# Scores of two batches from float32r parts, and smaller work for the engines beside TensorE

## The chip, the cores and the metric

The kernel runs on one core of one Trainium2 chip. The metric is the device time of one execution in microseconds (us). A core has TensorE (PE in the profile; PEld is its weight load), VectorE (DVE), ScalarE (ACT), GpSimd (POOL) and the queue that issues transfers (SP). Each engine takes its own instructions strictly in the order in which the program lists them.

## The reference

```
scores = 0.125 * q @ k.T            # 4 batches x 8 heads, 576 x 576, head size 64, float32
thresh = max(scores) - tau          # by row
attn   = exp(where(scores >= thresh, scores, -1e9) - max)
attn   = attn / (sum(attn) + 1e-9)
x      = attn @ v                   # then 2304 tokens of 512
x      = moe(x, rms_norm)           # silu(xn @ w_gate) * (xn @ w_val) @ w_out, 512 -> 1536 -> 512
out    = moe2(x)                    # the same without the norm
```

The weights of the two feed-forward layers arrive as 64-bit floats.

## The kernel before, in words

The work of a batch is 36 score tiles (4 pairs of heads, 9 tiles of 128 query rows a pair; the fifth tile of a pair is made of two halves of 64 rows, one from each head) and then 36 units of feed-forward work of 48 matmuls each. A dense matmul is `128x128` weights against 288 columns, and float32 accuracy comes from three products of float32r parts (`dense`, L614): each operand is held as a rounded part and a remainder.

The program is not written in the order in which it runs. `op(...)` records each step with an engine, a planner's cost, what it reads and writes, and a priority; `Program.order` lists the steps by a simulation of its own, and the instructions are then issued in that list's order. The tables at the top (`NORM_E`, `V_E`, `OFF` and so on) choose which engine takes a step and how early it stands. The result is this: the 36 tiles of batch 0 run first, alone (the front, to about 110 us); then the dense units of batch b run with the tiles of batch b+1 between them; the units of the last batch run alone. Between batches stands the RMS norm: sums (L495), a short chain on DVE (`tok`, L500 to L510) and a spreading product (L518), which starts at 138.6 us for batch 0 and at 1009.9 us for batch 3.

One score tile goes through these lines: L388 `QK` (PE, float32 operands straight from `raw`, the transposed q and k, stored twice: partitions 0 to 63 and again 64 to 127; each half of the 576 columns uses one of the copies), L411 row maximum (DVE), L412 thresholds and bias from `K2`, which holds tau (DVE), L413 exponential (ACT), L414 mask and row sum (DVE), L420 and L421 two small steps on the sums (DVE), L426 reciprocal (DVE), L331/333/335 normalise (POOL, DVE or ACT by `NORM_E`), L346/348/350 the float16 part (by `HI_E`), L354/355 the remainder (by `LO_E`), L360 a transposing transfer, L447/450 the product with v. In the front the scores rotate over three PSUM tiles (`ps`), later they have one.

A weight unit (`weights`) is converted once, from 64 bits to 32, for each of 36 units in the front and under batch 0: three ACT steps (L581, L582, L583) and one DVE step (L584). Then L586 (ACT) and L588 (DVE or POOL) make the two parts. `q` and `qu` in L576 are every second 16-bit word of a scratch tile `t`.

## Time and profile before

| what | value |
|---|---|
| time, median of 3 runs | 1258.54 us (1257.33 to 1258.66) |
| the profiled execution | 1255.49 us |
| its span, first to last instruction | 1253.7 us |
| granted TensorE clock, mean | 0.98 |
| PE busy | 1186.2 us, 95% |
| DVE, ACT, POOL busy | 739.3, 625.2 and 393.0 us |

The profiled execution lasted 1.8 us more than its span. "Busy" of PE is the time in which a matmul was in flight; since matmuls are pipelined, the durations of single ones overlap, and the distance from start to start tells more.

### The profile page before, as it was taken

What the parts mean: (1) busy time and instruction counts of PE and PEld (TensorE: products, weight loads), DVE (VectorE), ACT (ScalarE), POOL (GpSimd) and SP (SyncE); (2) the same over time, 40 slices, a digit from 0 to 9 for tenths busy, and PEclk for the clock granted to TensorE, in tenths of its full rate; (3) what the DMA queues carried; (4) which work ended last, traced back from release to release, by engine and by line L of the source; (5) the groups of instructions that cost most, each with busy time, mean ns of one, the idle gap of its engine ahead of it and who ended that gap; (6) DMA issues with size and microseconds to landing.
All of it is one profiled execution on the core that took longest, in us unless ns stands there. A gap on an engine that the chain in (4) does not pass through costs nothing.

```text
span 1253.7 us, 21723 instructions
## 1 busy us (share of the span) xinstructions
PE 1186.2 (95%) x8528; PEld 1052.7 (84%) x8528; DVE 739.3 (59%) x1643; ACT 625.2 (50%) x875; POOL 393.0 (31%) x399
## 2 busy tenths in 40 slices
PE   4766799899999999999999999999999999999998
PEld 2334688788888988988889988889888999999998
DVE  7796787767778876566646566456545341233122
ACT  4789879999999644324333234333334212112211
POOL 3676434538443413222131243214232110001010
PEclk9787799999999999999999999999999999999999
DMA  8789679999999998768866677677656554444442
GB/s 236 165 180 218 229 235 276 287 292 293 306 293 282 300 291 189 197 188 197 197 197 188 177 207 188 195 196 178 174 168 175 161 175 167 167 168 168 168 168 106
DMA packets 225656, 261.48 MB, mean 209 GB/s; under 512 B 195985, under 2 KB 196497, under 8 KB 202513
## 3 DMA queue, kind: packets, MB, share of 16 engines
q1 hardware_dynamic: 225552, 260.09, 73.6%
q8 instruction: 67, 1.10, 0.3%
q14 instruction: 37, 0.29, 0.1%
HBM read 175.11 MB, written 42.47 MB: 174 GB/s over the span
## 4 chain that ended last, share of the span: by engine, by line
PE 83%; ACT 5%; DVE 3%; issue 1%; DMA 1%; POOL 0%; ACTq 0%; DVEq 0%; POOLq 0%
PE ps L614 71%; PE ps L388 5%; PE pt L447 4%; PE pt L450 2%; ACT t L581 1%; ACT t L583 1%; ACT t L582 1%; DVE w L584 1%; DMA ag<-e 1%; ACT w L586 0%; PE ps L518 0%; ACT e L346 0%; ACT e L413 0%; DVE e L414 0%; ACT e L335 0%
## 5 line engine op out<-in xcount | busy, mean ns | idle before, releaser
L614 PEld LDWEIGHTS ps<-XS,w 128*128 128x128 f32 x4608 | 619.9, 189 | 44.3 <-issue 30.8
L614 PE MATMUL ps<-XS,w 128*128 128x288 f32 x4608 | 648.5, 299 | 7.6 <-ACT XS L542 2.3
L614 PE MATMUL ps<-h,w 128*128 128x288 f32 x2304 | 322.6, 296 | 2.8 <-DVE Y L700 1.8
L614 PEld LDWEIGHTS ps<-h,w 128*128 128x128 f32 x2304 | 307.6, 188 | 19.9 <-issue 15.6
L411 DVE TENSOR_REDUCE col<-ps 128x1 f32<-128x576 f32 x144 | 107.9, 753 | 100.8 <-PE ps L388 100.3
L668 ACT CAST h<-th 128x576 fp32r<-128x576 f32 x96 | 64.5, 672 | 201.7 <-DVE th L664 201.6
L671 POOL TENSOR_TENSOR h<-th,h 128x576 fp32r<-128x576 f32 x45 | 65.7, 1459 | 298.4 <-ACT h L668 298.4
L653 DVE SCALAR_TENSOR_TENSOR th<-th,ps 128x576 f32<-128x576 f32 x94 | 70.7, 752 | 136.2 <-ACT th L652 136.1
L388 PE MATMUL ps<-raw 64*128 64x288 f32 (+1 forms) x640 | 115.1, 480 | 34.8 <-DVE Y L414 16.4
L414 DVE SCALAR_TENSOR_TENSOR e<-ps,col,e 128x576 f32<-128x576 f32 x126 | 102.5, 814 | 63.5 <-ACT e L413 63.1
L652 ACT ACTIVATE th<-ps 128x576 f32<-128x576 f32 x94 | 61.2, 651 | 134.0 <-PE ps L614 133.3
L413 ACT ACTIVATE e<-ps,col 128x576 f32<-128x576 f32 x126 | 92.9, 737 | 61.6 <-DVE col L412 60.6
L664 DVE SCALAR_TENSOR_TENSOR th<-th,ps 128x576 f32<-128x576 f32 x94 | 70.6, 751 | 58.7 <-PE ps L614 58.3
L447 PE MATMUL pt<-ag,v 128*128 128x256 f16 (+1 forms) x576 | 89.7, 306 | 15.9 <-DMA ag<-e 9.6
L388 PEld LDWEIGHTS ps<-raw 64*128 64x128 f32 (+1 forms) x640 | 45.8, 187 | 69.0 <-DVE Y L414 23.2
L447 PEld LDWEIGHTS <-v 128*128 128x128 bf16 x576 | 54.4, 103 | 43.0 <-issue 18.6
L354 POOL TENSOR_TENSOR e<-e,e 128x512 f16<-128x512 f32 x68 | 80.8, 1188 | 0.0
L355 POOL TENSOR_TENSOR e<-e,e 128x64 f16<-128x64 f32 x68 | 27.0, 397 | 160.1 <-ACT e L346 111.5
L700 DVE SCALAR_TENSOR_TENSOR Y<-ps,Y 128x576 f32<-128x576 f32 x64 | 48.2, 755 | 46.5 <-PE ps L614 45.6
L346 ACT CAST e<-e 128x576 f16<-128x576 f32 x88 | 58.6, 666 | 27.1 <-POOL e L331 15.1
L335 ACT ACTIVATE e<-e,col 128x576 f32<-128x576 f32 x72 | 61.8, 858 | 13.4 <-DVE col L426 13.2
L588 POOL TENSOR_TENSOR w<-w,w 128x1024 fp32r<-128x1024 f32 x20 | 48.3, 2415 | 55.7 <-ACT w L586 45.1
(87 smaller groups left out, 999.7 us busy)
## 6 DMA issues: line engine op xcount, KB each, us to landing
w<-kept SPq DMA_DIRECT2D x108, 1024.0 KB, 5.3
w<-in_w SPq DMA_DIRECT2D x36, 1024.0 KB, 6.9
kept<-w SPq DMA_DIRECT2D x36, 1024.0 KB, 7.1
raw<-in_qkv SPq DMA_DIRECT2D x31, 576.0 KB, 6.0
v<-in_qkv SPq DMA_DIRECT2D x32, 160.0 KB, 4.8
...
```

The source lines that it names most:

```text
L335: op("ACT", 865, lambda: nc.scalar.activation(e, e, AF.Identity, bias=c[:, 4:5], scale=c[:, 3:4]), **k)
L354: op(en, 670 if eng == 2 else 1170, lambda: n1.tensor_tensor(h[:, 640:], e[:, :512], h[:, :512], ALU.subtract), lock=True, w=[("lo", n)], ...
L388: nc.tensor.matmul(s[m:m + w, j, :HS], x[k, c0:c0 + w], x[k, S + j * HS:S + (j + 1) * HS], start=True, stop=True)
L411: op("DVE", 745, lambda: nc.vector.tensor_reduce(c[:, 0:1], s2, AX.XY, ALU.max, negate=True), w=[sk, ("mx", n)], bufs=[cb], p=T + F['MAX'] ...
L413: op("ACT", 738, lambda: nc.scalar.activation(e2, s2, AF.Exp, bias=c[:, 2:3], scale=SCALE), r=[("thr", n)], w=[sk, ("e", n)] + ek, bufs=[c ...
L414: op("DVE", 890, lambda: nc.vector.scalar_tensor_tensor(e2, s2, c[:, 1:2], e2, ALU.is_ge, ALU.mult, accum_out=c[:, 6:7]), r=[("thr", n)], ...
L447: nc.tensor.matmul(pv_[:, :w], v12[:, i if i < 5 else i - 5], o[:, i, :w], start=(i == 0), stop=False)
L614: nc.tensor.matmul(pt[:, j, :HS], w(i, a), x(i, b_)[:, j * HS:(j + 1) * HS], start=(i == 0 and a == 0 and b_ == 0), stop=(i == n - 1 and a ...
L653: op("DVE", 745, lambda: nc.vector.scalar_tensor_tensor(t2, t2, 1.0, g2, ALU.add, ALU.mult), lock=raw, w=gk + [("th", n)], bufs=[tb], p=T ...
L664: op("DVE", 745, lambda: nc.vector.scalar_tensor_tensor(t2, t2, 0.5, v2, ALU.mult, ALU.mult), lock=raw, w=vk + [("th", n)], bufs=[tb], p=T ...
L668: op("ACT", 672, lambda: nc.scalar.copy(h[:, 0], tb.t), r=[("th", n)], w=[("h0", n)], bufs=[tb, hb], p=T + 2 * U + DRAIN + OFF['HH'], name ...
L671: op(eng, 720 if eng == "DVE" else 1430, lambda: n1.tensor_tensor(h[:, 1], tb.t, f32(h[:, 0]), ALU.subtract), lock=True, r=[("th", n), ("h ...
```

## The change

For heads 16 to 31 (batches 2 and 3) q and k are split into float32r parts ahead of their tiles, as the dense operands are. A new tile `sp` holds the rounded q (both copies), the remainder of q, and for k the rounded part above the remainder. Three copies (L334 on ACT, L332 on POOL) and two subtractions (L338 and L339) make it, for each head. A full tile of scores is then four matmuls: two of all 128 rows (rounded q against rounded k and its remainder at once) and two of 64 rows (remainder of q against rounded k), in place of two float32 matmuls of 64 rows. The half tiles stay as they were.

Which engine subtracts is told by the variable `n1`, which the same function sets again for the split of v before the recorded step is issued; so the table `V_E` decides it, and in the order of instructions 8 heads have both subtractions on VectorE and 8 on GpSimd, where the planner's own table (`Q_E`) has 5 and 11. The copies stand where they were planned, 41 on ScalarE and 7 on GpSimd.

Further: tau's transfer and its constant stand first; the two small steps on the sums move from DVE to POOL for batches 0 and 1 (`S_E`); the first two conversion steps work on packed 16-bit words, in the low half of the unit's 32-bit tile `w32`, and only the third writes every second word of `t`, of which there is one instead of two; small tiles are parts of one tile; and all tables and priorities have new numbers. So instructions stand in other places all through the program.

```diff
-HI_E = [(0, 1, 0, 2, 1, 1, 1, 1, 1), (0, 1, 1, 1, 1, 1, 0, 0, 1), (1, 2, 1, 1, 1, 1, 1, 1, 1)]
+HI_E = [(0, 0, 2, 1, 0, 1, 1, 0, 2), (2, 1, 0, 1, 0, 1, 0, 0, 1), (0, 2, 1, 1, 1, 1, 1, 1, 1)]
...
+FRH = 16
+S_E = (2, 0, 0)
+RAWN, SPN, TN = 4, 2, 1
...
+    r_s = ring("sp", SPN, [P, 3 * S + HS], F32R)
...
-    r_t = ring("t", 2, [P, 1024], U32)
+    r_t = ring("t", TN, [P, 1024], U32)
...
+        if hd >= FRH:
+
+            sp, rw = r_s.next(), raw[hd]
...
+                    op("ACT", 670 if i < 2 else 420, lambda o=o, y_=y_: nc.scalar.copy(o, y_), r=[(r, hd)], w=[(w, hd)], **k)
+            k["p"] = p + 1000
+            en, n1 = ("DVE", nc.vector) if 4 * hd + 3 in Q_E else ("POOL", nc.gpsimd)
+            c = 720 if en == "DVE" else 1430
+            op(en, c, lambda: n1.tensor_tensor(xs[:, S:2 * S], ys[:, :S], f32(xs[:, :S]), ALU.subtract), lock=True, r=[("rawq", hd), ("qh", hd)], w=[("ql", hd)], **k)
+            op(en, c, lambda: n1.tensor_tensor(xs[64:, 2 * S:3 * S], ys[:64, S:], f32(xs[:64, 2 * S:3 * S]), ALU.subtract), lock=True, r=[("rawk", hd), ("kh", hd)], w=[("kl", hd)], **k)
...
+                x = sp.t
                 for j in range(2):
-                    k = slice(64 * j, 64 * j + 64)
-                    nc.tensor.matmul(s[m:m + w, j, :HS], x[k, c0:c0 + w], x[k, S + j * HS:S + (j + 1) * HS], start=True, stop=True)
+                    nc.tensor.matmul(o[:, j], x[:, c0:c0 + w], x[:, 2 * S + j * HS:2 * S + (j + 1) * HS], start=True, stop=False)
+                nc.tensor.matmul(o[:, 0], x[:64, S + c0:S + c0 + w], x[:64, 2 * S:2 * S + HS], start=False, stop=True)
+                nc.tensor.matmul(o[:, 1], x[64:, S + c0:S + c0 + w], x[64:, 3 * S:], start=False, stop=True)
...
+        se = S_E[2 if fast else 1 if n < 2 * NTB else 0]
+        ns = nc.gpsimd if se == 0 else nc.vector
+
         def smalls():
-            nc.vector.tensor_scalar(cc(5), cc(6), 1e-9, 1.0 / UPP, ALU.add, ALU.mult)
-            nc.vector.tensor_scalar(cc(4), cc(6), 0.0, UPP / S, ALU.is_equal, ALU.mult)
+            ns.tensor_scalar(cc(5), cc(6), 1e-9, 1.0 / UPP, ALU.add, ALU.mult)
+            ns.tensor_scalar(cc(4), cc(6), 0.0, UPP / S, ALU.is_equal, ALU.mult)
...
-        q, qi, qu = [bb.t.bitcast(d)[:, 1::2] for d in (BF16, I16, U16)]
+        q, qi = w.bitcast(BF16)[:, :1024], w.bitcast(I16)[:, :1024]
+        qu = bb.t.bitcast(U16)[:, 1::2]
...
-    op("DMA", 625, lambda: nc.sync.dma_start(taus, tau), w=["tau0"], p=9000, name="tau")
+    op("DMA", 625, lambda: nc.sync.dma_start(taus, tau), w=["tau0"], p=-7500, name="tau")
```

Three places show how the order of instructions moves. The first is TensorE late under the third batch, with three tiles of scores of batch 3 among the dense matmuls (L614 before, L654 in the changed kernel; `ps_65` takes the scores, `XS`, `h` and `w` are dense operands). Before:

```order
L614 MATMUL ps_66<-XS,w_136 128x288 x18
L388 MATMUL ps_65<-raw_94 128x288 x2
L614 MATMUL ps_66<-XS,w_136 128x288 x6
L614 MATMUL ps_67<-XS,w_134 128x288 x24
L614 MATMUL ps_66<-XS,w_134 128x288 x18
L388 MATMUL ps_65<-raw_94 128x288 x2
L614 MATMUL ps_66<-XS,w_134 128x288 x6
```

In the changed kernel:

```order
L654 MATMUL ps_67<-XS,w_125 128x288 x12
L420 MATMUL ps_65<-sp_91 128x288 x2
L421 MATMUL ps_65<-sp_91 128x288
L422 MATMUL ps_65<-sp_91 128x288
L654 MATMUL ps_67<-XS,w_125 128x288 x12
L654 MATMUL ps_66<-XS,w_125 128x288 x24
L654 MATMUL ps_67<-XS,w_126 128x288 x12
L420 MATMUL ps_65<-sp_91 128x288 x2
L421 MATMUL ps_65<-sp_91 128x288
L422 MATMUL ps_65<-sp_91 128x288
```

Each tile now has its two full-row matmuls (L420) and its two 64-row ones (L421, L422) where one pair of float32 matmuls stood; the dense work around them keeps its pace of 48 to a tile.

The second is GpSimd at the start of the program, behind the constants (`K` and `small` hold tau's constant, `v` the split of v, `col` the sums of a pair of tiles, `e` and `Y` the exponentials). Before:

```order
L240 MEMSET K_82 128x1
L320 TENSOR_TENSOR v_96<-v_96 128x5x64
L722 TENSOR_SCALAR K_82<-taus 128x1
L320 TENSOR_TENSOR v_99<-v_96 128x320
L320 TENSOR_TENSOR v_97<-v_97 128x5x64
L320 TENSOR_TENSOR v_100<-v_97 128x320
L355 TENSOR_TENSOR e_106<-e_101,e_106 128x64
```

In the changed kernel:

```order
L246 MEMSET small 128x1
L762 TENSOR_SCALAR small<-small 128x1
L344 TENSOR_TENSOR v_93<-v_93 128x5x64
L344 TENSOR_TENSOR v_96<-v_93 128x320
L459 TENSOR_SCALAR col_127<-col_127 128x2
L460 TENSOR_SCALAR col_127<-col_127 128x2
L374 TENSOR_SCALAR e_102<-Y 128x576
L344 TENSOR_TENSOR v_97<-v_94 128x320
```

Tau's constant stands ahead of every split of v, and the two small steps on the sums (L459, L460) are now in this queue.

The third is VectorE in the same place (L411 and L447 are the row maxima, L412 and L448 the thresholds, L414 and L450 the masks, L426 and L465 the reciprocals). Before:

```order
L411 TENSOR_REDUCE col_108<-ps_65 128x1
L411 TENSOR_REDUCE col_108<-ps_66 128x1
L412 SCALAR_TENSOR_TENSOR col_108<-ps_65,col_108,K_82 128x2
L412 SCALAR_TENSOR_TENSOR col_108<-ps_66,col_108,K_82 128x2
L411 TENSOR_REDUCE col_109<-ps_67 128x1
L414 SCALAR_TENSOR_TENSOR Y,col_108<-ps_65,col_108,Y 128x576
L414 SCALAR_TENSOR_TENSOR e_101,col_108<-ps_66,col_108,e_101 128x576
L412 SCALAR_TENSOR_TENSOR col_109<-ps_67,col_109,K_82 128x2
L420 TENSOR_SCALAR col_108<-col_108 128x2
L421 TENSOR_SCALAR col_108<-col_108 128x2
L426 RECIPROCAL col_108<-col_108 128x2
```

In the changed kernel:

```order
L447 TENSOR_REDUCE col_127<-ps_65 128x1
L344 TENSOR_TENSOR v_95<-v_92 128x320
L448 SCALAR_TENSOR_TENSOR col_127<-ps_65,col_127,small 128x2
L447 TENSOR_REDUCE col_127<-ps_66 128x1
L448 SCALAR_TENSOR_TENSOR col_127<-ps_66,col_127,small 128x2
L450 SCALAR_TENSOR_TENSOR Y,col_127<-ps_65,col_127,Y 128x576
L447 TENSOR_REDUCE col_128<-ps_67 128x1
L450 SCALAR_TENSOR_TENSOR e_98,col_127<-ps_66,col_127,e_98 128x576
L448 SCALAR_TENSOR_TENSOR col_128<-ps_67,col_128,small 128x2
L447 TENSOR_REDUCE col_128<-ps_65 128x1
L465 RECIPROCAL col_127<-col_127 128x2
L448 SCALAR_TENSOR_TENSOR col_128<-ps_65,col_128,small 128x2
```

The two small steps ahead of the reciprocal are gone from this queue; two other instructions stand here between the mask that makes the pair's second sum and the reciprocal that needs GpSimd's result.

## Rows read from the trace of the kernel before

**Rows 1.** The page: busy us, share of the span and instructions of each engine.

```profile
PE 1186.2 (95%) x8528; PEld 1052.7 (84%) x8528; DVE 739.3 (59%) x1643; ACT 625.2 (50%) x875; POOL 393.0 (31%) x399
```

**Rows 2.** Four windows: busy us of PE, PEld, DVE, ACT, POOL; granted clock; DMA.

```profile
20.00:110.00 90.00, 58.66 (x321) 28.89 (x320) 77.51 (x218) 74.97 (x116) 60.44 (x74) 0.80 0.84 178
140.80:435.20 294.40, 284.26 (x2056) 249.59 (x2056) 229.59 (x456) 266.54 (x323) 138.97 (x116) 1.00 0.94 273
436.30:1009.90 573.60, 573.60 (x4199) 512.92 (x4199) 336.67 (x829) 208.33 (x331) 148.34 (x163) 1.00 0.72 193
1010.90:1253.70 242.80, 238.92 (x1797) 238.46 (x1795) 65.62 (x87) 42.37 (x64) 22.83 (x16) 1.00 0.46 162
```

**Rows 3.** Timeline of PE inside the second batch: start, us, matmuls.

```profile
593.82 0.76 PE L388 MATMUL ps<-raw 64*128 64x288 f32 x4
594.50 6.64 PE L614 MATMUL ps<-XS,w 128*128 128x288 f32 x48
601.08 0.76 PE L388 MATMUL ps<-raw 64*128 64x288 f32 x4
```

**Rows 4.** The chain that ended last: its share by line, and its last long piece.

```profile
by line: PE ps L614 70.7%; PE ps L388 5.4%; PE pt L447 4.1%; PE pt L450 1.8%; issue 1.4%; ACT t L581 0.9%; ACT t L583 0.8%; ACT t L582 0.7%; DVE w L584 0.7%; DMA ag<-e 0.5%; ACT w L586 0.5%; PE ps L518 0.4%; ACT e L346 0.4%; ACT e L413 0.4%
...
1011.10 238.73 PE ps L614 x1794
```

**Rows 5.** Groups by line and shape: count, busy us, mean ns of one, idle before.

```profile
L388 PE MATMUL ps<-raw 64*128 64x288 f32 x512 | 103.3, 488 | 31.7 <-DVE Y L414 16.0 <-DVE e L414 11.1 <-DMA raw<-in_qkv 4.5
...
L583 ACT ACTIVATE t<-t,half 128x1024 uint16<-128x1024 int16 x36 | 52.4, 1455 | 0.2
...
L581 ACT ACTIVATE t<-w 128x1024 bf16<-128x1024 bf16 x36 | 49.7, 1382 | 5.2 <-DMA w<-in_w 5.1
...
L582 ACT ACTIVATE t<-t 128x1024 bf16<-128x1024 bf16 x36 | 49.1, 1365 | 0.3
...
L586 ACT CAST w<-w 128x1024 fp32r<-128x1024 f32 x36 | 37.3, 1037 | 2.3 <-DVE w L584 2.3
...
L346 ACT CAST e<-e 128x576 f16<-128x576 f32 x88 | 58.6, 666 | 27.1 <-POOL e L331 15.1 <-DVE e L333 10.9 <-DMA ag<-e 0.2
...
L335 ACT ACTIVATE e<-e,col 128x576 f32<-128x576 f32 x72 | 61.8, 858 | 13.4 <-DVE col L426 13.2
...
L671 POOL TENSOR_TENSOR h<-th,h 128x576 fp32r<-128x576 f32 x45 | 65.7, 1459 | 298.4 <-ACT h L668 298.4
...
L420 DVE TENSOR_SCALAR col<-col 128x1 f32<-128x1 f32 x112 | 16.7, 149 | 2.1
...
L420 DVE TENSOR_SCALAR col<-col 128x2 f32<-128x2 f32 x16 | 6.9, 433 | 0.0
...
L421 DVE TENSOR_SCALAR col<-col 128x2 f32<-128x2 f32 x16 | 3.1, 195 | 0.0
...
L722 POOL TENSOR_SCALAR K<-taus 128x1 f32<-128x1 f32 x1 | 0.2, 192 | 0.1
```

**Rows 6.** Timeline of the start, from the loads to the first exponential.

```profile
4.12 0.52 SPq L721 DMA_DIRECT2D taus<-in_tau  x1
...
6.06 1.02 DVE L320 TENSOR_TENSOR v<-v 128x320 f32<-128x320 f32 x2 [3.06 <-DMA v<-in_qkv]
...
6.99 1.42 DVE L411 TENSOR_REDUCE col<-ps 128x1 f32<-128x576 f32 x2
...
10.07 0.72 POOL L320 TENSOR_TENSOR v<-v 128x320 f32<-128x320 f32 x1 [8.59 <-DMA v<-in_qkv]
...
10.88 0.19 POOL L722 TENSOR_SCALAR K<-taus 128x1 f32<-128x1 f32 x1
...
11.10 0.35 DVE L412 SCALAR_TENSOR_TENSOR col<-ps,col,K 128x2 f32<-128x2 f32 x2 [2.69 <-POOL K L722]
...
11.42 0.74 ACT L413 ACTIVATE Y<-ps,col 128x576 f32<-128x576 f32 x1 [9.05 <-DVE col L412]
```

**Rows 7.** Waits between 20 and 110 us: total, times, longest.

```profile
PE ps L388 <- DVE e L414: 11.4, 8, 2.8
```

More of the change, by code (lines that the diff above doesn't have):

```diff
@@ L229, in body @@
     make_identity(nc, ident)
-    ones = sb.tile([P, 2], F32, name="ones")
+    small = sb.tile([P, 46], F32, name="small")
+    ones = small[:, 30:32]
     nc.gpsimd.memset(ones, 1.0)
-    half = sb.tile([P, 1], F32, name="half")
+    half = small[:, 32:33]
     nc.gpsimd.memset(half, 2.0 ** 15)
-    taus = sb.tile([P, 1], F32, name="taus")
-    rgs = sb.tile([P, NC], F32, name="rgs")
-    K0, K2 = [sb.tile([P, 2], F32, name=f"K{i}") for i in (1, 2)]
+    taus = small[:, 33:34]
+    rgs = small[:, 34:38]
+    K0, K2 = small[:, 38:40], small[:, 40:42]
     nc.gpsimd.memset(K0[:, 0:1], -1.0)
@@ L266, in body @@
     r_w = ring("w", 3, [P, 2, 1024], F32R)
-    r_tok = ring("tok", 6, [P, 5], F32)
+    r_tok = Ring([small[:, 5 * i:5 * i + 5] for i in range(6)])
+    r_col = ring("col", 5, [P, 14], F32)
     def SU(u):
@@ L385, in QK @@
                 x = raw[hd].t
+                sp = SP.get(hd) if w == P else None
+                o = s[m:m + w, :, :HS]
+                if sp is None:
+                    for j in range(2):
+                        k = slice(64 * j, 64 * j + 64)
+                        nc.tensor.matmul(o[:, j], x[k, c0:c0 + w], x[k, S + j * HS:S + (j + 1) * HS], start=True, stop=True)
+                    continue
+                x = sp.t
                 for j in range(2):
-                    k = slice(64 * j, 64 * j + 64)
-                    nc.tensor.matmul(s[m:m + w, j, :HS], x[k, c0:c0 + w], x[k, S + j * HS:S + (j + 1) * HS], start=True, stop=True)
+                    nc.tensor.matmul(o[:, j], x[:, c0:c0 + w], x[:, 2 * S + j * HS:2 * S + (j + 1) * HS], start=True, stop=False)
+                nc.tensor.matmul(o[:, 0], x[:64, S + c0:S + c0 + w], x[:64, 2 * S:2 * S + HS], start=False, stop=True)
+                nc.tensor.matmul(o[:, 1], x[64:, S + c0:S + c0 + w], x[64:, 3 * S:], start=False, stop=True)
         r = []
-        for hd, *_ in parts:
-            if hd:
+        for hd, _, w, _ in parts:
+            if hd in SP and w == P:
+                r += [("qh", hd), ("ql", hd), ("kh", hd), ("kl", hd), ("kb", hd)]
+            elif hd:
                 r += [("rawq", hd), ("rawk", hd)]
@@ L395, in tile_ops @@
                 r += [("rawk", 0, 0), ("rawk", 0, 1), ("rawq", 0, 0), ("rawq", 0, 1)]
-        op("PE", 690 * len(parts), QK, r=r, w=[sk], bufs=[raw[hd] for hd, *_ in parts], p=T, name=f"QK{n}")
+        op("PE", sum(460 if hd in SP and w == P else 690 for hd, _, w, _ in parts), QK, r=r, w=[sk], bufs=[SP[hd] if hd in SP and w == P else raw[hd] for hd, _, w, _ in parts], p=T, name=f"QK{n}")
         if not second:
@@ L718, in moe @@
             outp(2)
[L721 to L722 removed]
+    op("DMA", 625, lambda: nc.sync.dma_start(taus, tau), w=["tau0"], p=-7500, name="tau")
+    op("POOL", 130, lambda: nc.gpsimd.tensor_scalar(K2[:, 0:1], taus, -1.0 / SCALE, 1.0, ALU.mult, ALU.mult), r=["tau0"], w=["tau"], p=-1e9, name="tau")
     for t, key in ((PA, "PA"), (PB, "PB"), (PD, "PD")):
```

45 lines of the change are left out of this document (26 added, 19 removed).

## The prediction

> **What bounds the kernel now.** I read the page first: TensorE is busy for 1186.2 of 1253.7 us, the next engine for 739.3 [rows 1]. That is an average over stages, so the windows came next. In the long stretch from the second norm to the fourth (436.3 to 1009.9 us), PE is busy for all of its 573.60 us at the full clock, while ACT has 208 and POOL 148 us of work [rows 2]. There nothing but PE's own work sets the time. Under batch 0 (140.8 to 435.2) PE is busy for 284.26 of 294.40 us, and ACT for 266.54, or 91% [rows 2]: PE sits idle for 10.1 us, and ACT is the engine that is nearly full. In the front (20 to 110) PE, DVE, ACT and POOL are busy for 58.66, 77.51, 74.97 and 60.44 of 90 us, at a mean clock of 0.80 [rows 2]; no engine is full, DVE is the fullest, and TensorE's scores wait for DVE's masks to free PSUM [rows 7]. The chain that ended last says the same: 70.7% dense matmuls, 5.4% scores, and of the rest the conversion steps L581 to L583 have 2.4%, or 30 us [rows 4].
>
> So three things can shorten the run: less PE work anywhere behind the front (one us for one us), less idle time of PE under batch 0, and an earlier end of the front. The sum is made against the profiled execution: 1255.49 us, of which 1253.7 is the span and 1.8 lies around it. The median of the runs is 3.05 us above that execution; I add the same difference to the result.
>
> **The scores on TensorE.** What a tile costs is read from starts, since durations overlap. From one tile of scores to the next, 48 dense matmuls between, it takes 601.08 - 593.82 = 7.26 us [rows 3]. Undisturbed, 1794 dense matmuls take 238.73 us, 0.1331 each [rows 4], so 48 take 6.39. A tile therefore costs 0.87 us: 0.68 from its start to that of the dense matmuls [rows 3], and 0.19 that these lose around it, in the change between 128-row and 64-row operands.
>
> The new form is not in this trace. Its two full-row matmuls have the shape and type of dense ones: 0.27. The 0.19 stays, because the last two matmuls still have 64 rows. Their price is open. The old pair shows four records a tile (512 for 128 full tiles [rows 5]); two float32 products in two passes each, one behind the other, would be those four at about 0.17, or 0.68. If the new pair overlaps in the two halves of the array it takes one pass, 0.13 to 0.17; if not, two, about 0.34. I take 0.20, near the overlapping end. Sum: 0.27 + 0.19 + 0.20 = 0.66, a saving of 0.21 a tile. There are 64 such tiles (16 heads, 4 full tiles each): **-13.5 us**. From below, with the loss at the change gone too: 0.27 + 0.13 = 0.40, or -30 us. From above: 0.27 + 0.34 + 0.26 (the loss, and a half more of it for a second start) = 0.87, no gain.
>
> Against dropping the 0.19 stands a rule. The Trainium skill, "TensorEngine Tiling (Array Packing)", section "Key Properties", says that a change of tiling mode drains TensorE. The 0.19 in rows 3 agrees; by the rule it is paid in both forms, and the gain of 30 us is out of reach.
>
> The split itself is new work: 3 copies and 2 subtractions for each of 16 heads. As bounds I take the 0.67 of a cast on ACT and the 1.46 of a subtraction on POOL [rows 5]: 41 copies on ACT are at most 27 us, 8 heads on POOL at most 23 us and the rest about half of that on DVE. It is spread from late in batch 0 to the end of batch 2, mostly over a stretch in which ACT and POOL have 365 and 425 us free [rows 2]. In the order of instructions a head's subtractions stand 4 to 6 tiles ahead of its first tile (about 30 us at 7.3 a tile), and two `sp` tiles leave room for that. I cost it at nothing; uncovered, on PE's path, it would be some 4 us a head, 64 in all.
>
> **Tau first.** The two first row maxima run from 6.99 on, yet the thresholds wait until 11.10 for the constant, which GpSimd makes at 10.88 behind a split of v, and the first exponential starts at 11.42 [rows 6]. Now the constant stands first on POOL and tau's transfer ahead of that of v. The first v had landed by 6.06 [rows 6]; what takes its place in the queue should land about then. The DVE queue has one maximum (0.71), half of v's split (0.51) and a threshold (0.2) before the exponential: about 8.9 with the v half a microsecond later. **-2.5 us**; bounds 0 (absorbed later) and -3.4.
>
> **The small steps.** Batch 0 has 16 pairs at 0.433 + 0.195 and 4 single tiles at twice 0.149, so 11.2 us leave DVE in the front [rows 5]. Batch 1 loses 36 times 0.30, or 11 us, under a DVE that is 78% busy [rows 2]. On POOL the nearest row is 0.192 for a 128x1 step [rows 5], thus 8 us more in the front and 14 under batch 1. Each result now goes DVE, POOL, DVE. Behind the reciprocal, which waits for it on DVE, stand the maxima and masks of later tiles, and PE waits for those.
>
> **The conversion.** The three ACT steps take 1.382, 1.365 and 1.455 us, but a copy of as many contiguous 32-bit values (L586) takes 1.037, and a cast of 576 to packed 16-bit words 0.666 [rows 5]. So 16-bit words in themselves cost nothing, and strided ones about a third of a microsecond. The second step, now packed on both sides, saves 0.33. Of the first (strided read, packed write) and the third (packed read, strided write) one should save as much, depending on which side costs: 0.66 a unit, bounds 0.33 and 1.0. For about 30 units under batch 0 that is 20 us of ACT time. The tables also take 16 normalisations (0.858) and some 9 casts (0.666) from ACT there [rows 5], 20 us more; splits of two heads give back 4. ACT falls from 91% to 79%. Most of PE's 10.1 us of idle time should go, not all, since PE also waits at this stretch's start while the norm and first units pass through ACT and DVE: **-6 us**, bounds 0 and -10.1.
>
> **The front.** DVE loses 11 of 77.5 us, ACT about 9 (four casts, two conversion steps of 18, and 0.22 on each of the rest). POOL gains 8 and some steps from the tables. If DVE alone set the pace, 11 us would go; with ACT nearly as full and the longer way through POOL I take a third: **-4 us**, bounds +4 and -12.
>
> Sum: -13.5 - 2.5 - 6 - 4 = -26. The profiled execution would be 1229.5 us, its span 1227.7, and the median 1258.5 - 26 = **1232.5 us**.
>
> **The rivals.** (1) The front gives nothing: POOL's queue delays the small steps by as much as DVE gains, and the idle time under batch 0 stays. For it: POOL is 67% busy in the front, and its steps last up to 1.46 us. Against it: two or more instructions of DVE usually stand between mask and reciprocal. Then only the scores count: 1245.
>
> (2) The new scores cost what the old ones did, because the 64-row pair doesn't overlap. Against it: the old pair's 0.68 leaves no room for eight dense-sized passes. Time: 1232.5 + 13.5 = 1246.
>
> (3) Packing changes nothing. The Trainium skill, "SBUF — State Buffer", section "Door 1: The DMA port swizzle", says that two accesses to a 16-byte line are enough for full bandwidth, so the old strides (4 and 8 bytes) would already be free. The rows speak against it (1.365 against 1.037 for the second step). If something else makes these steps slow, ACT keeps 20 us under batch 0, and the front and the idle time give back some 4: 1236.5.
>
> (4) Slower: the reciprocal stands at the head of DVE's queue while POOL is still in a long step, and everything behind it waits, PSUM stays full, PE idles. Each of the 20 reciprocals of the front would cost the rest of a step of POOL, up to 1.46 us and the two small steps. At 1.9 us each it is 38 in place of the 4 gained: 1258.5 - 22 + 38 = 1274. It decides against the change from 1.1 us a reciprocal (22 over 20). Against it: the two or more DVE instructions ahead of most reciprocals, 1 us or more.
>
> **How the numbers follow.** My forecast, 1220 to 1242, has 0.56; rival 1 has 0.14, rival 2 0.07, rival 3 0.07, rival 4 0.08; a larger gain (both better bounds of the scores and the front) 0.04, and rivals 1 and 2 together, no change, 0.04. The range 1217 to 1249 holds all but rival 4, no change, and half of the larger gain, somewhat more than 8 in 10. A measurement of this kernel can tell about 0.2%, 2.5 us, from no change: faster 0.88, same 0.04, slower 0.08.
>
> **What would show it.** In the profile after: four score records among dense matmuls, 7.26 us from tile to tile falling to about 7.05 in batches 2 and 3; no PE wait for `sp`; the first exponential near 9 us; the three conversion steps at 3.5 us together instead of 4.2; PE's idle time under batch 0 at about 4 us; the first norm's spread some 6 us earlier, with more dense work ahead of it. I am wrong if the distance from tile to tile doesn't fall, if DVE waits for POOL before its reciprocals, or if PE idles beyond 436 us, where it never does now.

## The result, and the profile after

The changed kernel takes **1240.87 us** (median of 4 runs, 1239.24 to 1243.21); before took 1258.12 in the same session (1257.33 to 1258.66). The ratio is 0.9859, 95% interval 0.984 to 0.9878. The forecast was 1232.5, its range 1217 to 1249. The profiled execution has a span of 1237.9 us in place of 1253.7: 15.8 us are gone (the medians differ by 17.3).

The page, busy us, share and instructions of each engine, against [rows 1]:

```profile
PE 1175.8 (95%) x8528; PEld 1058.3 (85%) x8528; DVE 749.5 (61%) x1566; ACT 598.0 (48%) x855; POOL 466.3 (38%) x566
```

TensorE lost 10 us of work, ACT 27, and POOL gained 73; which of that paid, only the stretches tell. The first three windows of [rows 2] follow, the second and third moved with the norms:

```profile
20.00:110.00 90.00, 59.33 (x326) 29.86 (x322) 72.15 (x172) 71.54 (x113) 68.84 (x112) 0.76 0.87 172
134.70:426.30 291.60, 281.28 (x2024) 247.72 (x2024) 233.36 (x404) 242.61 (x301) 165.82 (x201) 0.99 0.95 285
427.50:985.70 558.20, 557.15 (x4127) 510.80 (x4127) 347.15 (x841) 209.66 (x336) 190.58 (x205) 1.00 0.72 192
```

Under batch 0 ACT fell from 91% to 83% (79% was forecast), and yet PE is idle for 291.60 - 281.28 = 10.3 us, where it was idle for 10.1 before. From the second norm to the fourth PE waits for 558.20 - 557.15 = 1.05 us in all, where it waited for nothing.

The tile of scores, PE's timeline in the second batch, against [rows 3]:

```profile
590.77 0.43 PE L420 MATMUL ps<-sp 128*128 128x288 f32 x2
591.13 0.40 PE L421 MATMUL ps<-sp 64*128 64x288 f32 x1
591.13 0.40 PE L422 MATMUL ps<-sp 64*128 64x288 f32 x1
591.46 6.62 PE L654 MATMUL ps<-XS,w 128*128 128x288 f32 x48
597.91 0.42 PE L420 MATMUL ps<-sp 128*128 128x288 f32 x2
598.26 0.39 PE L421 MATMUL ps<-sp 64*128 64x288 f32 x1
598.27 0.40 PE L422 MATMUL ps<-sp 64*128 64x288 f32 x1
```

Tile to tile is 597.91 - 590.77 = 7.14 us, from 7.26. A tile costs 7.14 - 6.39 = 0.75 instead of 0.87, and not 0.66. The two 64-row products start together, so they do overlap; but the full-row pair takes 0.36 from its start to that of the 64-row pair, instead of the 0.27 of two dense matmuls, and the 64-row pair 0.33 until the dense work starts. The tile shown is a typical one: the median over such tiles behind the second norm is 0.87 before (39 tiles) and 0.75 after (36).

The start, and the groups by line and shape of the conversion and the small steps, against [rows 5, 6]:

```profile
5.39 0.19 POOL L762 TENSOR_SCALAR small<-small 128x1 f32<-128x1 f32 x1 [3.92 <-DMA small<-in_tau]
...
8.06 0.21 DVE L448 SCALAR_TENSOR_TENSOR col<-ps,col,small 128x2 f32<-128x2 f32 x1
...
8.37 0.74 ACT L449 ACTIVATE Y<-ps,col 128x576 f32<-128x576 f32 x1 [6.01 <-DVE col L448]
```

```profile
L623 ACT ACTIVATE t<-w,small 128x1024 uint16<-128x1024 int16 x36 | 52.6, 1461 | 0.3
L621 ACT ACTIVATE w<-w 128x1024 bf16<-128x1024 bf16 x36 | 41.0, 1140 | 12.3 <-DMA w<-in_w 11.2 <-DVE e L372 0.5 <-DVE w L628 0.5
L622 ACT ACTIVATE w<-w 128x1024 bf16<-128x1024 bf16 x36 | 37.9, 1054 | 0.4
...
L459 POOL TENSOR_SCALAR col<-col 128x1 f32<-128x1 f32 x40 | 17.9, 447 | 41.5 <-DVE e L450 33.7 <-DVE col L465 5.6
```

The first exponential is 3.05 us earlier. The three conversion steps take 3.66 us together instead of 4.20. The step that reads and writes packed words (L622) takes 1.05, and the one that reads strided and writes packed (L621) 1.14. The third (L623) now reads packed words, still writes every second one, and keeps its 1.46. In the first step (L621) only the written side changed and 0.24 us went, in the third only the side that is read and nothing went: the price lies on the side that is written. ACT's wait for the weights from HBM grows from 5.1 to 11.2 us: part of the saved time turns into waiting for a transfer. A 128x1 step on POOL takes 0.447 us, above the 0.192 row that priced it.

**Where the 15.8 us came from.** The norms cut the run into three stretches, at the starts of the spreading product (L518, L557; 138.62 and 435.24 before, 133.62 and 426.37 after). The number of dense matmuls in a stretch, counted in the order of instructions, differs (60, 1638 and 5214 before; 90, 1620 and 5202 after), so each is taken out at its 0.1331 us [rows 4]; what remains is everything else: waits, scores, products with v.

| us left without dense matmuls | front | under batch 0 | behind the second norm |
|---|---|---|---|
| before | 130.6 | 78.6 | 124.5 |
| after | 121.6 | 77.1 | 119.1 |
| difference | -9.0 | -1.5 | -5.4 |

So the stretch with the new tiles gave the smaller part, and the front the larger. These are single executions. Run 6 below has the median of before, yet its profiled span is 5.8 us longer than this one of before, all of it in the first two columns (2.4 and 3.5 us). Differences of 2 or 3 us in them carry nothing; those behind the second norm agree better (124.5 in both).

Part of the 9.0 is the clock's. TensorE around the first norm, before and then after, each with the window from 125 to 130 us (its granted clock is the third number from the end; 0.50 is the lower of its two levels, 1.2 GHz):

```profile
130.12 2.13 PE L495 MATMUL pt<-ones,SS 128*128 128x2 f32 x10
132.10 3.99 PE L614 MATMUL ps<-XS,w 128*128 128x288 f32 x18
138.62 2.40 PE L518 MATMUL ps<-ident,tok 128*128 128x128 f32 x10 [2.53 <-DVE tok L510]
...
125.00:130.00 5.00, 2.61 (x11) 1.78 (x12) 3.25 (x5) 3.53 (x6) 2.75 (x3) 0.50 0.97 342
```

```profile
126.95 1.17 PE L534 MATMUL pt<-small,SS 128*128 128x2 f32 x10
127.99 5.80 PE L654 MATMUL ps<-XS,w 128*128 128x288 f32 x42
133.62 1.23 PE L557 MATMUL ps<-ident,small 128*128 128x128 f32 x10
...
125.00:130.00 5.00, 4.60 (x37) 4.47 (x36) 3.16 (x10) 4.63 (x7) 0.00 (x0) 1.00 0.86 303
```

From the norm's sums to its spread it was 8.50 us with 18 dense matmuls, 6.1 without them; now it is 6.67 with 42, 1.1 without them. So 5.0 of the 9.0 us lie there: the 2.53 us in which TensorE waited for `tok` are now filled with dense work, and this execution kept the full clock. Run 5 below has the changed kernel's order and 0.50 in that window, and the same stretch takes 9.52 us, 2.9 more. So the front's gain at like clocks is uncertain: the fronts of runs 5 and 2 (0.60 there), 124.3 and 124.6, lie some 6 us below the 130.6 of before and 8.5 below the 133.0 of run 6, whose clock was low there too.

### The profile page after: what moved, and what is told of

Same layout as the page of the kernel before. It is cut to its first block, busy times and chain, and to the rows that moved or that the text cites. A ratio compares the mean times of both kernels' runs of the same rounds, so it can differ in the third digit from the quotient of the medians.

```text
span 1237.9 us, 21834 instructions
## 1 busy us (share of the span) xinstructions
PE 1175.8 (95%) x8528; PEld 1058.3 (85%) x8528; DVE 749.5 (61%) x1566; ACT 598.0 (48%) x855; POOL 466.3 (38%) x566
## 4 chain that ended last, share of the span: by engine, by line
PE 83%; DMA 6%; DVE 4%; ACT 3%; POOL 1%; issue 1%; SPq 0%; ACTq 0%; DVEq 0%; POOLq 0%
PE ps L654 70%; PE pt L486 5%; DMA ag<-e 4%; PE ps L415 3%; PE pt L489 2%; DMA w<-in_w 2%; PE ps L421 2%; PE ps L420 1%; DVE col L447 1%; ACT t L623 1%; DVE w L624 1%; POOL e L378 0%; DVE Y L450 0%; ACT e L449 0%; DVE e L450 0%
## 5 line engine op out<-in xcount | busy, mean ns | idle before, releaser
L654 PE MATMUL ps<-XS,w 128*128 128x288 f32 x4608 | 645.8, 297 | 10.1 <-DVE XS L588 3.8
L654 PEld LDWEIGHTS ps<-XS,w 128*128 128x128 f32 x4608 | 617.0, 188 | 35.8 <-issue 16.2
L654 PE MATMUL ps<-h,w 128*128 128x288 f32 x2304 | 320.3, 296 | 0.3 <-DVE th L693 0.3
L654 PEld LDWEIGHTS ps<-h,w 128*128 128x128 f32 x2304 | 307.2, 188 | 11.9 <-issue 8.1
L447 DVE TENSOR_REDUCE col<-ps 128x1 f32<-128x576 f32 x144 | 108.0, 753 | 75.4 <-PE ps L422 52.5
L693 DVE SCALAR_TENSOR_TENSOR th<-th,ps 128x576 f32<-128x576 f32 x94 | 70.7, 752 | 119.7 <-ACT th L692 119.6
L450 DVE SCALAR_TENSOR_TENSOR e<-ps,col,e 128x576 f32<-128x576 f32 x126 | 102.5, 814 | 38.6 <-ACT e L449 38.4
L486 PE MATMUL pt<-ag,v 128*128 128x320 f16 (+1 forms) x576 | 89.3, 305 | 23.2 <-DMA ag<-e 13.3
L378 POOL TENSOR_TENSOR e<-e,e 128x512 f16<-128x512 f32 x82 | 101.0, 1233 | 0.0
L415 PE MATMUL ps<-raw 64*128 64x288 f32 (+1 forms) x384 | 67.7, 511 | 24.6 <-DVE Y L450 14.4
L379 POOL TENSOR_TENSOR e<-e,e 128x64 f16<-128x64 f32 x82 | 31.1, 381 | 129.3 <-ACT e L370 51.9
L415 PEld LDWEIGHTS ps<-raw 64*128 64x128 f32 (+1 forms) x384 | 27.7, 195 | 49.2 <-DVE Y L450 20.8
L374 POOL TENSOR_SCALAR e<-e 128x576 f16<-128x576 f32 x50 | 36.0, 720 | 73.7 <-DVE e L357 41.3
L503 ACT ACTIVATE pvt<-pt 64x320 f32<-64x320 f32 (+1 forms) x64 | 25.8, 405 | 68.6 <-PE pt L489 68.0
L711 DVE TENSOR_TENSOR h<-th,h 128x576 fp32r<-128x576 f32 x53 | 46.9, 885 | 18.4 <-ACT h L708 18.3
```

Source lines behind the costliest of these rows:

```text
L378: op(en, 670 if eng == 2 else 1170, lambda: n1.tensor_tensor(h[:, 640:], e[:, :512], h[:, :512], ALU.subtract), lock=True, w=[("lo", n)], ...
L415: nc.tensor.matmul(o[:, j], x[k, c0:c0 + w], x[k, S + j * HS:S + (j + 1) * HS], start=True, stop=True)
L447: op("DVE", 745, lambda: nc.vector.tensor_reduce(c[:, 0:1], s2, AX.XY, ALU.max, negate=True), w=[sk, ("mx", n)], bufs=[cb], p=T + F['MAX'] ...
L450: op("DVE", 890, lambda: nc.vector.scalar_tensor_tensor(e2, s2, c[:, 1:2], e2, ALU.is_ge, ALU.mult, accum_out=c[:, 6:7]), r=[("thr", n)], ...
L486: nc.tensor.matmul(pv_[:, :w], v12[:, i if i < 5 else i - 5], o[:, i, :w], start=(i == 0), stop=False)
L654: nc.tensor.matmul(pt[:, j, :HS], w(i, a), x(i, b_)[:, j * HS:(j + 1) * HS], start=(i == 0 and a == 0 and b_ == 0), stop=(i == n - 1 and a ...
```

## The experiments

There were two theories at the start. A: the scores gained too little because the 64-row pair still changes the row tiling, and the small edits (tau, small sums, packing) each gave their part of the front. Rival: the small edits give nothing by themselves, and the front's gain is the new order that the tables make. The runs are of two kinds: those that keep the order of instructions on every engine, and those in which the planner orders anew. The table that follows the runs has the three stretches of all of them.

**1. All four products over 128 rows** (same order; the last two now multiply the remainder of q with both parts of k).

```diff
-                nc.tensor.matmul(o[:, 0], x[:64, S + c0:S + c0 + w], x[:64, 2 * S:2 * S + HS], start=False, stop=True)
-                nc.tensor.matmul(o[:, 1], x[64:, S + c0:S + c0 + w], x[64:, 3 * S:], start=False, stop=True)
+                for j in range(2):
+                    nc.tensor.matmul(o[:, j], x[:, S + c0:S + c0 + w], x[:, 2 * S + j * HS:2 * S + (j + 1) * HS], start=False, stop=True)
```

> The changed kernel with the last two products of a tile of scores over all 128 rows (remainder of q against both parts of k, one product more than needed), everything else in the same order on every engine. Theory A: a tile costs 0.75 us in the changed kernel because the 64-row pair makes TensorE change its tiling and back; four matmuls like dense ones then cost 4 x 0.133 = 0.53 us, 0.22 less in 64 tiles, so 14 us less than the change: about 1227 us, and 48 dense matmuls with a tile take 6.92 us from tile to tile. Rival B: the cost lies in four products and their weights whatever the rows; then only the pair's 0.33 falls to 0.27, 4 us in all: about 1237.

Measured 1224.13 us (1220.39 to 1226.1), ratio 0.9717 [0.9699, 0.9735]. PE's timeline of this kernel, two tiles with 36 dense matmuls between:

```profile
561.60 0.43 PE L420 MATMUL ps<-sp 128*128 128x288 f32 x2
561.86 0.42 PE L422 MATMUL ps<-sp 128*128 128x288 f32 x2
562.13 4.92 PE L654 MATMUL ps<-h,w 128*128 128x288 f32 x36
566.89 0.43 PE L420 MATMUL ps<-sp 128*128 128x288 f32 x2
```

566.89 - 561.60 - 36 x 0.1331 = 0.50 us a tile, a quarter of a microsecond less than in the changed kernel, with twice the rows in the last pair. Over the 36 tiles that stand so the median is 0.49. 64 x 0.25 = 16 of the 16.7 us by which the medians of the runs differ; rival B had 4. By starts, 0.10 of the 0.25 lies ahead of the last pair (0.36 against 0.26), 0.06 in it (0.33 against 0.27) and 0.09 in the dense matmuls behind (6.45 - 6.39 in the change, 4.76 - 4.79 here). So most of the loss lies where 128-row and 64-row operands meet; why TensorE loses time there, no run shows.

**2. The old float32 products in the changed kernel** (the splits are still made and not used; the scores read buffers that later loads may have overwritten).

```diff
-                x = sp.t
                 for j in range(2):
-                    nc.tensor.matmul(o[:, j], x[:, c0:c0 + w], x[:, 2 * S + j * HS:2 * S + (j + 1) * HS], start=True, stop=False)
-                nc.tensor.matmul(o[:, 0], x[:64, S + c0:S + c0 + w], x[:64, 2 * S:2 * S + HS], start=False, stop=True)
-                nc.tensor.matmul(o[:, 1], x[64:, S + c0:S + c0 + w], x[64:, 3 * S:], start=False, stop=True)
+                    k = slice(64 * j, 64 * j + 64)
+                    nc.tensor.matmul(o[:, j], x[k, c0:c0 + w], x[k, S + j * HS:S + (j + 1) * HS], start=True, stop=True)
```

> The changed kernel with the old float32 products of 64 rows for all scores; the split parts are still made but not used, and the order on all other engines is that of the change. Theory A: the new scores are worth the 0.12 us a tile that starts show (0.87 against 0.75), so the time rises by 7.7 us to about 1248.5. Rival B: the scores gave nothing and the gain comes from the front alone: about 1241. Rival C: they were worth the 13.5 us of the prediction: 1254.

Measured 1250.09 (1248.97 to 1251.81), ratio 0.9927 [0.9914, 0.994]: 9.2 us above the change. Not all of it is the products. Waits of PE behind the second norm, total, times, longest:

```profile
PE ps L420 <- DMA raw<-in_qkv: 4.8, 4, 1.7
```

Here PE itself waits for the loads; in the change the splits meet them, off PE. With the waits taken out on both sides (4.8 us here, 1.05 in the change), the products differ by 9.5 (128.6 - 119.1 in the table) - 4.8 + 1.05 = 5.8 us, nearest to theory A.

**3. Strided conversion steps** (the first two steps write and read every second 16-bit word again; same order).

```diff
-        q, qi = w.bitcast(BF16)[:, :1024], w.bitcast(I16)[:, :1024]
+        q, qi = w.bitcast(BF16)[:, 1::2], w.bitcast(I16)[:, 1::2]
```

> The changed kernel with the first two conversion steps on every second 16-bit word again, in the same buffers and the same order. Theory A: ScalarE gets 20 us of work back under batch 0 and some 5 in the front, and TensorE waits for it: 3 to 8 us slower, 1244 to 1249. Rival B: ScalarE no longer bounds either stretch, and the packing is worth nothing: 1241, within 1 us.

Measured 1242.85 (1237.38 to 1244.41), ratio 0.9862 [0.9844, 0.988]. The median is 2 us above the change's, between the two theories; the ratios, each against before in its own session, are the same (0.9862 and 0.9859). The steps are back at their old lengths, and the window under batch 0 shows ACT with 14 us more work:

```profile
L621 ACT ACTIVATE w<-w 128x1024 bf16<-128x1024 bf16 x36 | 49.6, 1379 | 8.3 <-DMA w<-in_w 7.5 <-DVE w L628 0.5
L622 ACT ACTIVATE w<-w 128x1024 bf16<-128x1024 bf16 x36 | 49.2, 1367 | 0.4
```

```profile
134.70:426.30 291.60, 279.14 (x2012) 245.23 (x2012) 234.79 (x401) 256.55 (x301) 164.91 (x201) 0.99 0.94 284
```

256.55 against 242.61 us of ACT, yet the stretch is only 1.7 us longer (78.8 against 77.1), within what single executions differ by. ACT being nearly full was not what left PE idle there.

**4. The small sums back on VectorE** (same places).

```diff
-        ns = nc.gpsimd if se == 0 else nc.vector
+        ns = nc.vector
```

> The changed kernel with the two small steps on the sums issued on VectorE for all batches, at the places in the program's order at which GpSimd had them; the planner still counts them as GpSimd's, so every other instruction keeps its place. Theory A: taking these 11 us off VectorE in the front (and 11 under batch 0) is what made the front end earlier, so their return costs 3 to 8 us: 1244 to 1249. Rival B: the way through GpSimd loses as much as VectorE gains, since a product with v waits 6.3 us for a small step there: 1241 or less.

Measured 1239.11 (1237.19 to 1241.67), ratio 0.9848 [0.9827, 0.9869]. That is rival B: their move to GpSimd gives nothing. The profiled front was 3.2 us shorter without it, which is no more than single executions differ by.

**5. Tau held back.** GpSimd first copies a scratch tile ten times, so that the constant comes late; otherwise the same order.

```diff
-    op("POOL", 130, lambda: nc.gpsimd.tensor_scalar(K2[:, 0:1], taus, -1.0 / SCALE, 1.0, ALU.mult, ALU.mult), r=["tau0"], w=["tau"], p=-1e9, name="tau")
+    op("POOL", 130, lambda: [nc.gpsimd.tensor_copy(RB[:, c:min(c + P, S)], ident[:, :min(P, S - c)]) for c in range(0, S, P)] and [nc.gpsimd.tensor_scalar(RB, RB, 1.0, 1.0, ALU.mult, ALU.mult) for _ in range(10)] and nc.gpsimd.tensor_scalar(K2[:, 0:1], taus, -1.0 / SCALE, 1.0, ALU.mult, ALU.mult), r=["tau0"], w=["tau"], p=-1e9, name="tau")
```

> The changed kernel, same order on every engine, but GpSimd first copies a scratch tile ten times (0.82 us each, after five copies of at most 128 columns), so that tau's constant comes at about 10.8 us instead of 5.39 and the first exponential at about 11.3 instead of 8.37, as before the change. Theory A: the early start passes through to the end, so the time rises by 2.5 to 3.0 us, to about 1243.6. Theory B: the front absorbs it, since its masks, products and splits are nearly as full a little later: within 1.2 us of 1240.9.

Measured 1242.65 (1236.43 to 1244.99), ratio 0.986 [0.9831, 0.9889]. The median is 1.8 us above the change's, between the two theories, but the ratio is the change's (0.9859), and its interval is too wide to part them. PE's timeline around the first norm tells more. The changed kernel has its last product with v here, and its sums and spread as shown above:

```profile
118.27 1.16 PE L486 MATMUL pt<-ag,v 128*128 128x256 f16 x9
```

This kernel, with the window from 125 to 130 us:

```profile
116.39 1.16 PE L486 MATMUL pt<-ag,v 128*128 128x256 f16 x9
...
126.73 2.13 PE L534 MATMUL pt<-small,SS 128*128 128x2 f32 x10
128.71 7.70 PE L654 MATMUL ps<-XS,w 128*128 128x288 f32 x42
136.25 1.23 PE L557 MATMUL ps<-ident,small 128*128 128x128 f32 x10
...
125.00:130.00 5.00, 5.00 (x24) 5.00 (x23) 2.17 (x7) 4.12 (x6) 0.00 (x0) 0.50 0.72 259
```

Though the first exponential is at 11.20 instead of 8.37, the last product with v comes 1.9 us earlier and the norm's sums (L534) 0.2 earlier: the front has absorbed the delay. What makes the spread later is TensorE's clock: the same sums take 2.13 us instead of 1.17 and the same 42 matmuls 7.70 instead of 5.80, with a granted clock of 0.50 instead of 1.00 from 125 to 130 us. The edit need not be the reason: in run 2, where tau is early, the sums take 2.13 us too. So the profile speaks for theory B; run 6 tests the same thing with more runs.

**6. Tau first in the kernel before** (same order but for the transfer and the constant).

```diff
-        op("DMA", 600, lambda: nc.sync.dma_start(v.t[:, :, 0], qkv[b, h, :, 2 * S:].rearrange("p (c d) -> p c d", c=5)), w=[("v1", hd)], bufs=[v], p=p + 1000, name=f"load{hd}")
+        op("DMA", 600, lambda: (hd == 0 and (nc.sync.dma_start(taus, tau), nc.gpsimd.tensor_scalar(K2[:, 0:1], taus, -1.0 / SCALE, 1.0, ALU.mult, ALU.mult)), nc.sync.dma_start(v.t[:, :, 0], qkv[b, h, :, 2 * S:].rearrange("p (c d) -> p c d", c=5))), w=[("v1", hd)], bufs=[v], p=p + 1000, name=f"load{hd}")
-    op("DMA", 625, lambda: nc.sync.dma_start(taus, tau), w=["tau0"], p=9000, name="tau")
-    op("POOL", 130, lambda: nc.gpsimd.tensor_scalar(K2[:, 0:1], taus, -1.0 / SCALE, 1.0, ALU.mult, ALU.mult), r=["tau0"], w=["tau"], p=9000, name="tau")
+    op("DMA", 625, lambda: None, w=["tau0"], p=9000, name="tau")
+    op("POOL", 130, lambda: None, r=["tau0"], w=["tau"], p=9000, name="tau")
```

> The kernel before, same order on every engine, except that tau's transfer stands ahead of the first v on SP and its constant ahead of the split of v on GpSimd. The first exponential should start near 8.9 us instead of 11.42. Theory A: the 2.5 us reach the end: 1255.8. Theory B: they are absorbed: 1257.5 to 1259. In no case the +14 us that the same edit cost when it was free to change the order; if it does cost that, the early constant itself hurts and not the order.

Measured 1258.29 (1255.17 to 1261.27), ratio 0.9994 [0.9978, 1.0009]. The first exponential starts at 9.00 instead of 11.42, and the time is 0.5 us below that of before in the same session (1258.80): theory B, the gain is absorbed.

**7. The same edit, free to change the order.** Only the priorities of tau's two steps are the change's; the planner then moves hundreds of other instructions.

```diff
-    op("DMA", 625, lambda: nc.sync.dma_start(taus, tau), w=["tau0"], p=9000, name="tau")
+    op("DMA", 625, lambda: nc.sync.dma_start(taus, tau), w=["tau0"], p=-7500, name="tau")
-    op("POOL", 130, lambda: nc.gpsimd.tensor_scalar(K2[:, 0:1], taus, -1.0 / SCALE, 1.0, ALU.mult, ALU.mult), r=["tau0"], w=["tau"], p=9000, name="tau")
+    op("POOL", 130, lambda: nc.gpsimd.tensor_scalar(K2[:, 0:1], taus, -1.0 / SCALE, 1.0, ALU.mult, ALU.mult), r=["tau0"], w=["tau"], p=-1e9, name="tau")
```

> The kernel before with tau's transfer and constant first, as in the change, and nothing else; the planner then orders other instructions anew. Theory A: the first exponential starts 3 us earlier and the front ends as much earlier: 1256. Rival B: the gain is lost in the front's other waits: 1259. If the time moves by more than 3 us either way, the new order did it, not tau.

Measured 1273.43 (1272.74 to 1275.84), ratio 1.0126 [1.0104, 1.0148]: 14 to 15 us slower, though the constant comes at 5.32 us, as early as in run 6 (5.48). The order did it. Waits of PE from 140 to 440 us in this kernel follow; before had 2.4 us of the first kind:

```profile
PE ps L388 <- DVE e L414: 9.7, 7, 3.2
PE ps L614 <- DVE th L653: 4.4, 3, 3.4
```

**8. The kernel before with the change's tables** (engines, offsets and stage starts, no line of code).

> The kernel before with the tables, priorities and offsets of the change and none of its other edits. Theory A: the front's 9 us come from the new numbers: about 1250. Rival B: these numbers serve the edits (fewer steps on VectorE, shorter conversion) and without them gain nothing or lose: 1259 or more.

Measured 1269.48 (1267.13 to 1273.23), ratio 1.0091 [1.0067, 1.0114]: 10 us slower, which is rival B.

**9. The changed kernel with the old tables** (those for splits and sums, which the old have not, stay).

> The changed kernel with the numbers that the kernel before had for engines, offsets and stage starts (those for the new splits and sums stay the change's). Theory A: the four edits keep their price whatever the order, so scores (8.9) and tau (2.5) still pay and only the rest of the front's gain is gone: about 1247. Theory B: a planned order fits only the code that it was chosen for, and numbers from another kernel lose 10 us or more, as in the two runs of before that changed its order: 1252 to 1265.

Measured 1259.24 (1256.5 to 1263.14), ratio 1.0007 [0.9991, 1.0024]. That is theory B: without its numbers the change gives nothing. By stretches and against before, the scores still pay (119.8 instead of 124.5), but 9.3 us are lost under batch 0 (87.9 instead of 78.6), and of the front's 9.0 only 1.5 are left.

**10. The first norm asked for earlier** (by its due time; the planner orders anew).

```diff
-        T = SU(36 * b) - 3000 + 0
+        T = SU(36 * b) - (16000 if b == 0 else 3000)
```

> The changed kernel with the priority of the first norm's parts (the copies and subtractions into XS) 13 us earlier, so that on VectorE the subtractions stand ahead of the scaling of the first two units. Theory A: TensorE's idle 3.8 us at 138 us, when it waits for the first of these subtractions behind four scaling steps of 0.67 us, shrinks by 2.7 us: about 1238. Rival B: the first units' results come later by as much and TensorE stops for them in turn: 1241.

Measured 1250.49 (1246.61 to 1253.58), ratio 0.993 [0.9915, 0.9944]: about 10 us slower than the change, which neither theory had. The front is the same (122.9). The wait that the edit aimed at shrank from 3.8 to 0.8 us, but 12 us are lost under batch 0, where PE now waits for masks (4.1 us), transposes (3.7) and the gate's steps on VectorE (3.6).

**11. Full rows from batch 1 on, without the third copy** (the planner orders anew).

```diff
-FRH = 16
+FRH = 8
...
-            for i, (r, w, o, y_) in enumerate((("rawq", "qh", xs[:, :S], ys[:, :S]), ("rawk", "kh", xs[:64, 2 * S:3 * S], ys[:64, S:]), ("rawk", "kb", xs[64:, 3 * S:], ys[64:, S + HS:]))):
+            for i, (r, w, o, y_) in enumerate((("rawq", "qh", xs[:, :S], ys[:, :S]), ("rawk", "kh", xs[:64, 2 * S:3 * S], ys[:64, S:]))):
...
```

The rest of the edit is run 1's products, a smaller `sp` tile and the planner's cost of a tile of scores (530 for 460).

> The changed kernel with all four products of a tile over 128 rows, without the third copy of k, and with the split form for batch 1 too (heads 8 to 15), whose tiles run among the dense units of batch 0. The 1224 us of the full-row form are the base. Theory A: 32 more tiles save 0.35 us each on TensorE and the other engines carry the splits: 1213 to 1218. Rival B: under batch 0 the splits come late or push other steps back, and TensorE waits for as much as it saves: 1222 or more.

Measured 1244.79 (1242.86 to 1247.92), ratio 0.9898 [0.9878, 0.9917]: 20.7 us above run 1, though it has 32 more of the cheap tiles: rival B's side. Behind the second norm it equals run 1; the front lost 9.5 and batch 0 lost 7.7.

**12. Full rows, no third copy, small sums on VectorE** (run 1's order and products, run 4's edit; the third copy goes on both engines that make it, of which the lines on ScalarE are shown).

```diff
...
-                    op("ACT", 670 if i < 2 else 420, lambda o=o, y_=y_: nc.scalar.copy(o, y_), r=[(r, hd)], w=[(w, hd)], **k)
+                    op("ACT", 670 if i < 2 else 420, lambda o=o, y_=y_, i=i: nc.scalar.copy(o, y_) if i < 2 else None, r=[(r, hd)], w=[(w, hd)], **k)
...
```

> The changed kernel with its last two score products over all 128 rows, the third copy of each split left out (these products don't read it), and the small sums on VectorE at the same places; otherwise the same order. Theory A: copies and small steps are covered, so it is the full-row form alone, 1222.5 to 1225. Theory B: ACT's and GpSimd's relief (16 copies of about 0.43, some 110 small steps) and the shorter way to the reciprocal give 2 us or more on top: below 1222.

Measured 1225.17 (1222.9 to 1228.67), ratio 0.9732 [0.9707, 0.9757]: run 1's time again, within the noise. That is theory A: copies and small steps are covered. The best version measured is run 1, 1.4% below the change.

The stretches of all runs, worked out as above from the starts of the two spreading products and the span (same order as the change unless marked *; run 6 has the order of before):

| run | spreads at | span | front | batch 0 | behind |
|---|---|---|---|---|---|
| 1 full rows | 133.29, 427.00 | 1224.2 | 121.3 | 78.1 | 104.8 |
| 2 old products | 136.58, 429.04 | 1250.0 | 124.6 | 76.8 | 128.6 |
| 3 strided | 133.85, 428.23 | 1242.5 | 121.9 | 78.8 | 121.9 |
| 4 sums on DVE | 130.41, 423.39 | 1235.4 | 118.4 | 77.4 | 119.6 |
| 5 tau held | 136.25, 428.76 | 1242.9 | 124.3 | 76.9 | 121.8 |
| 6 tau, order of before | 140.97, 441.04 | 1259.5 | 133.0 | 82.1 | 124.5 |
| 7 tau * | 143.62, 449.11 | 1271.0 | 135.6 | 85.9 | 129.5 |
| 8 new tables * | 146.25, 450.52 | 1271.4 | 135.9 | 88.6 | 126.9 |
| 9 old tables * | 140.27, 442.98 | 1256.8 | 129.1 | 87.9 | 119.8 |
| 10 norm earlier * | 134.88, 438.25 | 1248.6 | 122.9 | 89.3 | 116.4 |
| 11 from batch 1 * | 143.60, 444.27 | 1241.1 | 130.8 | 85.8 | 104.4 |
| 12 full, DVE | 132.67, 425.39 | 1222.4 | 120.7 | 77.1 | 104.6 |

Every run in the change's order has a front of 118 to 125 and 77 to 79 under batch 0, whatever was done to its steps. Every run with an order of its own (*) lies 8 to 12 us above the change under batch 0, and all but run 10 lie 7 to 14 above it in the front. Runs 7 and 8 have the code of before; against before they lose 5 in the front and 7 and 10 under batch 0.

## Why the prediction was right, and where its terms were off

**The scores, -13.5.** The mechanism holds (the form is cheaper, the split is hidden: PE never waits for `sp`), the size does not. By starts it is 7.26 - 7.14 = 0.12 a tile, 7.7 us in 64; the stretch shows 5.4, or 6.5 without the new wait of 1.05; run 2 shows 5.8. So the term came out at half its size, for two reasons: the 64-row pair costs 0.33 until the next start and not 0.20, and the full-row pair 0.36 and not 0.27. Of the 0.19 that the dense matmuls lost around a tile, only 0.06 is left (6.45 - 6.39). The prediction weighed the Trainium skill, "TensorEngine Tiling (Array Packing)", section "Key Properties", by which a change of tiling mode drains TensorE. Run 1, which has no such change in these tiles, agrees: 0.50 a tile, no more than four dense matmuls. Rival 2, no gain, is out.

**Tau, -2.5.** Its step in the start was nearly right (8.37, forecast 8.9), its price wrong: run 6 shows that 2.4 us at the first exponential don't reach the end, and the profile of run 5 agrees with 2.8. That was the lower bound, "absorbed later".

**Small steps and the front, -4.** The front gave 9.0 us where tau and this term together had 6.5. But run 4 shows that it isn't the small steps, run 6 that it isn't tau, and run 3 (121.9 against 121.6) that it isn't the conversion. Rival 1, a front that gives nothing, is out. Rival 4 isn't seen either: VectorE waits for POOL before its reciprocals five times, 2.2 us in all, 0.8 at the longest. TensorE's longest wait in the front, 6.3 us before a product with v, is put down to a small step on POOL (L460), but run 4, without these steps on POOL, has it too (6.4 us, put down to VectorE's L508). The forecast let the loads of single engines set the front. In the runs the numbers alone lose 10 us (run 8), the code alone gives nothing (run 9), and only both together give 17. So what is left as the cause is the order as a whole, with the choice of engines that goes with it. That is argued by taking the single edits out one at a time; no run takes them all out with the order held, the joining of the small tiles into one was not tested, and which of the numbers matter is not settled. The last product with v comes at 118.27 instead of 123.83 (a wait of 3.91 us for a transposed tile stood before it). The first norm's spread is 5.0 us earlier with 30 more dense matmuls ahead of it, near the 6 that were forecast, but the 2.9 us of the clock are in it.

**The conversion, -6.** The steps came as forecast (3.66, forecast 3.5), ACT fell, and PE's idle time stayed at 10 us: the step "most of PE's idle time should go" failed. Run 3 gives ACT 14 us of work back, and the time hardly moves. So the stretch wasn't bound by ACT, and the idle time stays as in rival 3, but by another way than rival 3 said: packing does make the steps shorter (the second takes 1.37 strided in run 3 and 1.05 packed). The Trainium skill, "SBUF — State Buffer", section "Door 1: The DMA port swizzle", says that two accesses to a 16-byte line are enough for full bandwidth. These steps don't agree with it, and the measurement decides.

The trace of before already spoke against this term. TensorE's waits under batch 0 (140.8 to 435.2 us; total, times, longest) end at VectorE's steps for 7.8 us and at ACT's for 1.0 (the last link of each wait; what held VectorE up is not in these rows):

```profile
PE ps L388 <- DVE e L414: 2.4, 3, 1.2
PE ps L614 <- DVE th L664: 1.9, 2, 1.1
PE ps L614 <- DVE Y L700: 1.8, 1, 1.8
PE ps L614 <- DVE th L653: 1.7, 2, 1.4
...
PE ps L614 <- ACT Y L661: 0.6, 1, 0.6
PE ps L614 <- ACT XS L547: 0.4, 1, 0.4
```

The forecast took the busiest engine of the stretch for the one that TensorE waits for. In the changed kernel the longest wait there comes right behind the first norm, and the three largest of 10.3 us again end at VectorE:

```profile
PE ps L654 <- DVE XS L588: 3.8, 1, 3.8
PE ps L415 <- DVE e L450: 1.9, 3, 0.8
PE ps L654 <- DVE w L628: 1.5, 1, 1.5
```

The stretches give -9.0 in the front, -1.5 under batch 0 and -5.4 behind it, 15.8 us by the spans, where -26 was forecast. The direction was right by its mechanism: the scores are cheaper. The range was met by luck. Of the terms, only the scores paid in the way that was forecast, 5.4 to 7.7 us; with nothing else the time would be 1250 to 1253 (an estimate from 1258.1), outside the range. The rest came mostly from the front, through the order as a whole, which no term of the sum had. Of the signs of being wrong, PE's idle time beyond 436 us appeared, at 1.05 us, and so did VectorE's waits for POOL before its reciprocals, at 2.2.
